# Attention scores in seven blocks of 64 rows with both heads stacked, in a kernel of causal attention and a gated product

## The chip, the cores and the metric

The kernel runs on one core of a Trainium2 chip. The metric is device time in microseconds (us) of one execution; the median of several runs counts. The core has TensorE (PE in the rows; its weight loads are PEld), VectorE (DVE), ScalarE (ACT), GpSimd (POOL) and a queue that issues the DMA transfers (SP).

## What is computed

Causal attention over 4 batches, 12 heads, 448 positions and 64 columns a head; its output, 768 columns a position, goes through a gated product.

```python
# q, k, v: (4, 12, 448, 64)
scores = np.matmul(q, k.transpose(0, 1, 3, 2)) / np.sqrt(64)
scores = np.where(np.triu(np.ones((448, 448), bool), k=1), -1e9, scores)
scores = scores - scores.max(-1, keepdims=True)
attn = np.exp(scores); attn = attn / (attn.sum(-1, keepdims=True) + 1e-9)
x = concat_heads(np.matmul(attn, v))              # (4 * 448, 768)
out = ((x @ w_a) * (x @ w_b)) @ w_out             # w_a, w_b: (768, 1536)
```

## The kernel before

**Numbers.** Everything is float32 at the output. Attention uses float32 matmuls. In the gated product each operand is split into a high and a low part and three products are summed (w_hi x_hi, w_hi x_lo, w_lo x_hi), each of 128 x 448 (line 586, 2484 of them in all). Weights arrive as 64-bit numbers and are converted by VectorE and ScalarE (lines 319 to 331), a unit of 128 x 768 at a time, then split (w_hi, w_lo).

**Order of the work.** The program is planned in one list of operations with estimated durations; a list scheduler (`Plan`) emits them in its own order, and each engine then runs its queue strictly in that order. First come batches 0 and 1, twelve pairs of heads (two heads share the 128 partitions of q and k, 64 each), with a few weight conversions in between. Each pair ends with `x_hi` (ScalarE) and `x_lo` (VectorE), its 128 rows of x. Then the products of batches 0 and 1 run, and the attention of batches 2 and 3, again twelve pairs, is set between them, a pair for every 30 groups of three products. Last come the products of batches 2 and 3, in a form with seven block products in place of eight; at that time the rooms of the attention (p, pt and others) hold parts of x.

**One pair.** `scores` makes, for each head, four row blocks: rows 0 to 63 against 64 columns, then three of 128 rows against 192, 320 and 448 columns (starts `QS`, ends `QE`). The two heads of a step are two matmuls on the two row halves of TensorE (64 rows each, 128 columns of weights), into two banks: s0 and s1 for the blocks of 448 and 64 columns, two m banks (batches 0 and 1) or t0 and t1 (batches 2 and 3) for 320 and 192. VectorE scales, adds the mask, writes to P and takes the row maximum in one instruction (line 409), ScalarE takes the exponential with its row sum (line 415). The sums go through an addition and a reciprocal on VectorE (lines 429 and 432), four of each a pair in batches 0 and 1 (`APART`), one of each later, on 128 x 8. P is then multiplied with them on GpSimd in batches 0 and 1 (line 442), on ScalarE later. The statistics have two tiles each, one a pair.

`turn` transposes P for one head: ten 128 x 128 pieces (line 464), in two banks t0 and t1, each then copied to a `pt` tile by ScalarE or VectorE (lines 268, 276). Where the diagonal piece's halves lie swapped, the `swapped` identity undoes it. `values` multiplies with V (line 484): four steps a head, weights of 64 columns, both heads at once on two column halves, into the bank pv.

**Rooms.** P lies in three rooms `p0` to `p2` of 128 x 1280, one a head. There are six `pt` tiles, four a pair; three V tiles; four tiles `raw` for q and k. The moving operands of the products are set 16 elements into their tiles (`SHIFT`).

**Start.** `START = "0w1ww"` orders the first loads: pair 0, a weight unit, pair 1, two units. Fillers (line 821) keep TensorE busy up to the first scores.

Of the kernel before, what the change touches and what calls it, by code (L numbers as in the profile page):

```python
# [18 lines left out]
P = 128  # L19
# [9 lines left out]
SHIFT, LINE = 16, 64  # L29

QS = (0, 64, 192, 320)
QE = (64, 192, 320, 448)
PO = (0, 128, 384, 768)
PW = 1280
NEG = -8.0e9

APART = (3, 3, 0, 0)
# [13 lines left out]
START = "0w1ww"  # L51
# [168 lines left out]
def causal_attention_then_gated_product(  # L220
# [18 lines left out]
    def shifted(tag, n, count, width):  # L239
        return plan.ring(tag, n, lambda i: sbuf.tile([P, LINE + count * width], F32R, tag=f"{tag}{i}", name=f"{tag}{i}")[  # L240
            :, SHIFT:SHIFT + count * width].rearrange("p (k f) -> p k f", k=count))
# [14 lines left out]
    sm_buf = [const.tile([P, 2, 4], F32, name=f"sm{i}") for i in range(2)]  # L256
# [34 lines left out]
    nth = [0, 0, 0]  # L291
# [80 lines left out]
    def scores(b, hp):  # L372
        qk_t = qk.pop((b, hp))
        sm = plan.ring("sm", 2, None)
        sm.tile = sm_buf[hp % 2]
        nm, rc = sb("nm", 2, [P, 2, 4]), sb("rc", 2, [P, 2, 4])
        for j in range(2):
            p = plan.ring("p", NPB, None)
            p.tile = p_buf[nth[0] % NPB]
            nth[0] += 1  # L380
            p_of[b, hp, j] = p

        def chunk(p, i):
            r = D if i == 0 else P
            return p.t[:r, PO[i]:PO[i] + QE[i]]

        for pair, w0 in (((3, 0), 448), ((2, 1), 320)):

            banks = [bank(f"s{j}") if w0 == 448 else bank("m", 3) if b < 2 else bank(f"t{j}") for j in range(2)]
            at = {pair[0]: slice(0, w0), pair[1]: slice(w0, 512)}  # L390
            for i in pair:

                def mm(i=i, banks=banks, at=at):
                    for j in range(2):
# [4 lines left out]
                    return r  # L399

                plan.op("pe", pe_ns(QE[i], 4) + 60, mm, [(qk_t, 0), (qk_t, 1)], banks)
            for j in range(2):
                p = p_of[b, hp, j]
                for i in pair:
                    r = D if i == 0 else P

                    def negmax(i=i, j=j, p=p, r=r, bk=banks[j], at=at):
                        m = mask[:r, 320:384] if i == 0 else mask[:, S - QE[i]:]
                        return nc.vector.tensor_tensor_reduce(  # L409
                            out=chunk(p, i), in0=bk.t[:r, at[i]], in1=m, scale=-0.125, scalar=3.0e38,  # L410
                            op0=ALU.add, op1=ALU.min, accum_out=nm.t[:r, j, i:i + 1],
                        )

                    def exp(i=i, j=j, p=p, r=r):
                        return nc.scalar.activation(  # L415
                            chunk(p, i), chunk(p, i), AF.Exp, bias=nm.t[:r, j, i:i + 1], scale=-1.0,
                            accum_out=sm.t[:r, j, i:i + 1],
                        )

                    plan.op("dve", dve_ns(QE[i]) + 10, negmax, [banks[j], "mask"], [(p, i), (nm, j, i)])  # L420
                    plan.op("act", act_ns(QE[i], False, 2), exp, [(nm, j, i)], [(p, i), (sm, j, i)])
        pairs = {slice(0, 4): (3, 0, 2, 1)}
        if APART[b] & 2:
            pairs = {slice(0, 4, 3): (3, 0), slice(1, 3): (2, 1)}
        heads = {slice(j, j + 1): (j,) for j in range(2)} if APART[b] & 1 else {slice(0, 2): (0, 1)}
        for si, ci in pairs.items():
            for sj, cj in heads.items():
                n = len(ci) * len(cj)
                plan.op("dve", 69 + n, lambda sj=sj, si=si: nc.vector.tensor_scalar_add(  # L429
                    rc.t[:, sj, si], sm.t[:, sj, si], 1.0e-9),  # L430
                    [(sm, j, i) for j in cj for i in ci], [(rc, j, i) for j in cj for i in ci])
                plan.op("dve", 115 + n, lambda sj=sj, si=si: nc.vector.reciprocal(  # L432
                    rc.t[:, sj, si], rc.t[:, sj, si]), [], [(rc, j, i) for j in cj for i in ci])
        for ci in pairs.values():
            for j in range(2):
                for i in ci:
                    def norm(i=i, j=j, p=p_of[b, hp, j]):
                        s = rc.t[:D if i == 0 else P, j, i:i + 1]
                        pc = chunk(p, i)
                        if NORM[b] == "act":  # L440
                            return nc.scalar.activation(pc, pc, AF.Copy, scale=s)
                        return nc.gpsimd.tensor_scalar(  # L442
                            out=pc, in0=pc, scalar1=s, scalar2=1.0, op0=ALU.mult, op1=ALU.mult
                        )

                    ns = act_ns(QE[i]) if NORM[b] == "act" else pool_ns(QE[i])
                    plan.op(NORM[b], ns, norm, [(rc, j, i)], [(p_of[b, hp, j], i)])


    spots = (((3, 448), (0, 0)), ((2, 320), (1, 0)))  # L450

    def turn(b, hp, j):
        p = p_of.pop((b, hp, j))
        for n, spot in enumerate(spots):
            t = bank(f"t{n}")
            for c, o in spot:
                for i in range(c, 4):


                    swap = c == i and c in (1, 2)  # L460
                    at = o + QS[i] - 128 * c + (D if swap else 0)

                    def mm(c=c, i=i, swap=swap, at=at, t=t):
                        return nc.tensor.matmul(  # L464
                            t.t[:, at:at + P],
                            p.t[:, PO[i] + 128 * c:PO[i] + 128 * (c + 1)],
                            swapped if swap else ident, is_transpose=True, start=True, stop=True,
                        )

                    plan.op("pe", 109, mm, [(p, i), "ident"], [t])  # L470
            full = sb("pt", 6, [P, 512])
            copy(TAKE[b][n], 512, lambda full=full: full.t, lambda t=t: t.t, [t], [full], True)
            pt[j, n] = full

    def values(b, hp, x):
        ps, vt = bank("pv"), v_of.pop((b, hp))
        parts = dict(pt)
        for c in range(4):
            n = 0 if c in (0, 3) else 1
            o = dict(spots[n])[c]  # L480

            def mm(c=c, n=n, o=o):
                for j in range(2):
                    r = nc.tensor.matmul(  # L484
                        ps.t[j * D:(j + 1) * D, 128 * c:S], vt.t[:, c, j, :],
                        parts[j, n].t[:, o:o + S - 128 * c], start=c == 0, stop=c == 3,
                    )
                return r

            plan.op("pe", pe_ns(S - 128 * c, 4) + 60, mm,  # L490
                    [(vt, 1 if c == 3 else 0), parts[0, n], parts[1, n]], [ps])
# [17 lines left out]
    def places(tag, n, take, count, width):  # L509

        at = SHIFT if tag == "pt" else LINE - SHIFT
        t = plan.ring(tag, n, lambda i: sbuf.tile([P, width], F32R, tag=f"{tag}{i}", name=f"{tag}_x{i}"))
        return [((lambda c=c: t.t[:, at + c * S:at + (c + 1) * S]), (t, c)) for c in range(take)]

    def make_rooms():
# [5 lines left out]
        block["T2"] = [[*places("p", 3, 2, 2, PW), *places("pt", 6, 1, 1, 512)] for _ in range(2)]  # L521
        block["T4"] = [[*places("p", 3, 2, 2, PW), *places("pt", 6, 1, 1, 512)]]

    def more_rooms():
        block["T4"].append(places("w_64", 3, 3, 3, 2 * UW))
        block["T3"] = [places("w_64", 3, 3, 3, 2 * UW) for _ in range(2)]
# [49 lines left out]
    def part_g(b, f, g, key):  # L576
        b, f = b % 2, f % HF
        copy("act", S, lambda: g_hi[:, b, f, :], g, [key], [("g_hi", b, f)])
        two_input("dve", S, lambda: g_lo[:, b, f, :], g,
                  lambda: g_hi[:, b, f, :].bitcast(F32), ALU.subtract, [key, ("g_hi", b, f)], [("g_lo", b, f)])  # L580
# [227 lines left out]
    for t in sm_buf:  # L808
        nc.vector.memset(t, 1.0)
# [72 lines left out]
```

## Time and profile before

| | |
|---|---|
| median of 3 runs | 677.49 us (677.25 to 677.79) |
| the profiled execution | 679.13 us |
| its span | 677.4 us |
| PE busy | 666.7 us (98%) |
| DVE busy | 474.7 us (70%) |
| ACT busy | 365.6 us (54%) |
| POOL busy | 56.0 us (8%) |
| chain that ended last | PE 90%, DVE 5%, ACT 3%, POOL 2% |

The span is what the rows add up to; the execution's own time has 1.7 us around it. Matmul records overlap, since they are pipelined, so a busy PE is not PE at its peak: its work is read from start to start. The same holds for short instructions of VectorE, whose records overlap by some tens of ns. Shapes stand as partitions x columns, out first; a matmul of float32 counts as two records.

### The profile page before, as it was taken

How to read it: one execution, taken by the hardware profiler on the slowest of the kernel's cores; microseconds unless marked ns; L12 is line 12 of the kernel's file. 1: busy time of each engine (PE TensorE's matmuls, PEld its weight loads, DVE VectorE, ACT ScalarE, POOL GpSimd, SP SyncE). 2: the span in 40 equal slices, each digit the busy share in tenths (PEclk: the TensorE clock that was granted, in tenths of full speed). 3: DMA queues.
4: the chain of work that ended last, by engine and by line, in shares of the span. 5: the costliest groups of instructions: out<-in, count | busy, mean ns of one | idle time of the engine just before them, and what ended most of it. 6: DMA issues, size and time to landing. Idle time of an engine off the chain costs nothing.

```text
span 677.4 us, 10680 instructions
## 1 busy us (share of the span) xinstructions
PE 666.7 (98%) x3754; PEld 578.6 (85%) x3754; DVE 474.7 (70%) x1122; ACT 365.6 (54%) x886; POOL 56.0 (8%) x107
## 2 busy tenths in 40 slices
PE   8999999999999999999999999999999999999997
PEld 6665568898898889889889889999999999999997
DVE  6889898898976665576767697478864237886521
ACT  5787767667657747757756753244432334343200
POOL 4455650000000000000000000000000000000000
PEclk9999999999999999999999999999999999999999
DMA  8335445657554764643542156412223231222542
GB/s 305 120 86 176 108 144 178 219 172 251 196 187 145 264 233 165 223 163 112 179 160 85 54 171 208 139 47 71 59 61 132 101 116 48 70 54 79 165 122 95
DMA packets 41716, 95.84 MB, mean 141 GB/s; under 512 B 4800, under 2 KB 27840, under 8 KB 41664
## 3 DMA queue, kind: packets, MB, share of 16 engines
q1 hardware_dynamic: 41664, 95.18, 42.5%
q8 instruction: 29, 0.48, 0.3%
q14 instruction: 23, 0.19, 0.1%
HBM read 67.24 MB, written 27.92 MB: 140 GB/s over the span
## 4 chain that ended last, share of the span: by engine, by line
PE 90%; DVE 5%; ACT 3%; POOL 2%; issue 1%; POOLq 0%; ACTq 0%
PE m L586 73%; PE t L464 6%; PE pv L484 4%; PE s L396 3%; ACT p L415 2%; DVE p L409 2%; POOL p L442 2%; PE t L396 2%; PE fill L821 1%; DVE pt L276 1%; DVE rc L429 1%; PE m L396 1%; ACT pt L268 1%; DVE w_m L321 0%; DVE rc L432 0%
## 5 line engine op out<-in xcount | busy, mean ns | idle before, releaser
L586 PE MATMUL m<-x_hi,w_hi 128*128 128x448 f32 x432 | 160.3, 371 | 0.0
L586 PE MATMUL m<-x_lo,w_hi 128*128 128x448 f32 x432 | 156.4, 362 | 0.0
L586 PE MATMUL m<-x_hi,w_lo 128*128 128x448 f32 x432 | 156.2, 362 | 0.0
L415 ACT ACTIVATE p<-p,nm 128x448 f32<-128x448 f32 (+1 forms) x192 | 95.0, 497 | 37.1 <-DVE nm L409 37.1
L284 DVE TENSOR_TENSOR w_lo<-w,w_hi 128x768 fp32r<-128x768 f32 (+1 forms) x84 | 65.8, 784 | 61.2 <-ACT w_hi L268 60.2
L586 PE MATMUL m<-g_hi,w_hi 128*128 128x448 f32 x288 | 105.3, 366 | 0.0
L586 PE MATMUL m<-g_lo,w_hi 128*128 128x448 f32 x288 | 104.3, 362 | 0.0
L586 PE MATMUL m<-g_hi,w_lo 128*128 128x448 f32 x288 | 104.0, 361 | 0.0
L268 ACT ACTIVATE w_hi<-w 128x768 fp32r<-128x768 f32 (+1 forms) x84 | 59.2, 704 | 67.8 <-PE m L586 54.8
L586 PEld LDWEIGHTS m<-x_hi,w_hi 128*128 128x128 f32 x432 | 81.1, 188 | 6.7 <-issue 0.9
L586 PEld LDWEIGHTS m<-x_hi,w_lo 128*128 128x128 f32 x432 | 80.9, 187 | 5.9
L586 PEld LDWEIGHTS m<-x_lo,w_hi 128*128 128x128 f32 x432 | 81.1, 188 | 4.5
L268 ACT ACTIVATE mid<-m 128x448 f32<-128x448 f32 x72 | 38.9, 540 | 80.4 <-PE m L586 67.6
L464 PE MATMUL t<-ident,p 128*128 128x128 f32 x384 | 65.9, 282 | 4.0 <-ACT pt L268 2.4
L284 DVE TENSOR_TENSOR mid<-m,acc 128x448 f32<-128x448 f32 x48 | 29.9, 624 | 45.5 <-PE m L586 45.1
L464 PEld LDWEIGHTS t<-ident,p 128*128 128x128 f32 x384 | 47.3, 142 | 14.1 <-POOL p L442 5.5
L586 PEld LDWEIGHTS m<-g_hi,w_hi 128*128 128x128 f32 x288 | 54.1, 188 | 3.9
L586 PEld LDWEIGHTS m<-g_hi,w_lo 128*128 128x128 f32 x288 | 53.9, 187 | 3.9
L442 POOL TENSOR_SCALAR p<-p,rc 128x320 f32<-128x320 f32 (+2 forms) x96 | 53.1, 569 | 45.2 <-ACT p L415 24.9
L586 PEld LDWEIGHTS m<-g_lo,w_hi 128*128 128x128 f32 x288 | 54.1, 188 | 3.0
L268 ACT ACTIVATE pt<-t 128x512 f32<-128x512 f32 x72 | 41.6, 594 | 24.4 <-PE t L464 24.1
L484 PEld LDWEIGHTS pv<-pt,v 128*64 128x64 f32 x384 | 25.8, 136 | 25.6 <-issue 17.2
(83 smaller groups left out, 982.0 us busy)
## 6 DMA issues: line engine op xcount, KB each, us to landing
w<-w SPq DMA_DIRECT2D x36, 768.0 KB, 4.5
w_keep<-w SPq DMA_DIRECT2D x36, 384.0 KB, 2.7
w<-w_keep SPq DMA_DIRECT2D x36, 384.0 KB, 3.0
raw<-qT SPq DMA_DIRECT2D x24, 224.0 KB, 3.1
raw<-kT SPq DMA_DIRECT2D x24, 224.0 KB, 3.4
o_keep<-mid SPq DMA_DIRECT2D x24, 224.0 KB, 2.1
acc<-o_keep SPq DMA_DIRECT2D x24, 224.0 KB, 2.7
out<-mid SPq DMA_DIRECT2D x24, 224.0 KB, 1.9
```

The source lines that it names most:

```text
L268: return nc.scalar.activation(o(), i(), AF.Copy)
L276: return nc.vector.tensor_copy(o(), i())
L284: plan.op(engine, ns, lambda: e.tensor_tensor(out=o(), in0=a(), in1=b(), op=op), reads, writes)
L396: r = nc.tensor.matmul(banks[j].t[:, at[i]], q[:, QS[i]:QS[i] + P], k[:, 0:QE[i]], start=True, stop=True)
L409: return nc.vector.tensor_tensor_reduce(out=chunk(p, i), in0=bk.t[:r, at[i]], in1=m, scale=-0.125, scalar=3.0e38, op0=ALU.add, op1=ALU.min ...
L415: return nc.scalar.activation(chunk(p, i), chunk(p, i), AF.Exp, bias=nm.t[:r, j, i:i + 1], scale=-1.0, accum_out=sm.t[:r, j, i:i + 1],)
L429: plan.op("dve", 69 + n, lambda sj=sj, si=si: nc.vector.tensor_scalar_add(rc.t[:, sj, si], sm.t[:, sj, si], 1.0e-9), [(sm, j, i) for j in ...
L442: return nc.gpsimd.tensor_scalar(out=pc, in0=pc, scalar1=s, scalar2=1.0, op0=ALU.mult, op1=ALU.mult)
L464: return nc.tensor.matmul(t.t[:, at:at + P], p.t[:, PO[i] + 128 * c:PO[i] + 128 * (c + 1)], swapped if swap else ident, is_transpose=True, ...
L484: r = nc.tensor.matmul(ps.t[j * D:(j + 1) * D, 128 * c:S], vt.t[:, c, j, :], parts[j, n].t[:, o:o + S - 128 * c], start=c == 0, stop=c == 3,)
L586: r = nc.tensor.matmul(ps.t[:, :S], a[:, i, :], x(), start=first and n == 0, stop=last and n == 2, skip_group_check=part)
L821: nc.tensor.matmul(fill[:, 0:S - SHIFT], warm[:, 0:P], warm[:, at:at + S - SHIFT], start=True, stop=True)
```

## The change

**Scores.** A pair has seven blocks of 64 rows, r = 0 to 6, with 64 (r + 1) columns. Both heads of a block are stacked: one head's 64 rows in partitions 0 to 63, the other's in 64 to 127 (swapped in odd blocks). Blocks are made two at a time, (6, 5), then 0 alone, in s0 and s1; then (4, 3) and (2, 1) in two other banks. A step of two blocks is four matmuls, on four 64 x 64 quadrants of TensorE. Row maximum, exponential and normalisation then take both heads in one instruction, seven of each a pair instead of eight; the statistics lie in one tile `st`, and there is one addition and one reciprocal a pair everywhere.

**Transposes.** A 128 x 128 piece holds both heads: 16 a pair instead of 20, in four banks as before; the copies write the two heads apart.

**Rooms.** P has one room of 128 x 2048 a pair. In batches 0 and 1 there are four, two of which lie where g_hi lies later (`early`); `close_front` makes the first writers of g_hi wait for the users of all four. Then there are two. `pt` has three tiles of twice the size. SHIFT is gone.

**Start.** Three pairs are loaded first, then three weight units; the fillers are float32 matmuls of 128 columns.

```diff
-START = "0w1ww"
+START = "012www"
...
-    NPB, NVB = 3, 3
+    NPB, NPF, NVB = 2, 4, 3
+    st_buf = [sbuf.tile([P, 3, 8], F32, tag=f"st{i}", name=f"st{i}") for i in range(2)]
...
-    g_hi = const.tile([P, 2, HF, S], F32R, name="g_hi")
+    early = sbuf.tile([P, 2 * HF * S], F32, tag="g_hi", name="early")
+    g_room = Buf(lambda: sbuf.tile([P, 2, HF, S], F32R, tag="g_hi", name="g_hi"), [])
...
+    def p_room(b):
+        if b < 2:
+            p = plan.ring("front", NPF, None)
+            n = (front[1][0] - 1) % NPF
+            p.tile = p_buf[n] if n < NPB else early[:, (n - NPB) * PW:(n - NPB + 1) * PW]
+        else:
             p = plan.ring("p", NPB, None)
...
-                def mm(i=i, banks=banks, at=at):
-                    for j in range(2):
-                        q, k = (qk_t.t[j * D:(j + 1) * D, h] for h in range(2))
-                        r = nc.tensor.matmul(
-                            banks[j].t[:, at[i]], q[:, QS[i]:QS[i] + P], k[:, 0:QE[i]], start=True, stop=True
-                        )
+                def mm(rs=rs, at=at):
+                    for r in rs:
+                        for j in range(2):
+                            to = j if r % 2 == 0 else 1 - j
+                            q, k = (qk_t.t[j * D:(j + 1) * D, h] for h in range(2))
+                            x = nc.tensor.matmul(at[r][0].t[to * D:(to + 1) * D, at[r][1]],
+                                                 q[:, r * D:(r + 1) * D], k[:, 0:D * (r + 1)], start=True, stop=True)
...
+        plan.op("dve", 165, lambda: nc.vector.tensor_scalar_add(st.t[:, rc, 0:NR], st.t[:, sm, 0:NR], 1.0e-9),
+                [(st, sm, r) for r in rows], [(st, rc, r) for r in rows])
...
+    groups = (((0, 0, 7), (3, 7, 1)), ((1, 0, 5), (2, 5, 3)))
+
+    def turn(b, hp, n):
+        p = p_of[b, hp]
+        full = sb("pt", 3, [P, 2, 8, D])
+        places = [(c, r) for c, o, count in groups[n] for r in range(2 * c, NR)]
+        for h in range(2):
+            t = bank(f"t{h}")
+            for i, (c, r) in enumerate(places[4 * h:4 * h + 4]):
...
+                        t.t[:, P * i:P * (i + 1)], p.t[:, PO[r] + P * c:PO[r] + P * (c + 1)],
+                        swapped if r % 2 else ident, is_transpose=True, start=True, stop=True,
...
-        nc.tensor.matmul(fill[:, 0:S - SHIFT], warm[:, 0:P], warm[:, at:at + S - SHIFT], start=True, stop=True)
+    plan.filler = lambda: nc.tensor.matmul(fill[:, 0:P], warm, warm, start=True, stop=True)
```

In the program's order, TensorE's scores of a pair of batch 2, between products, stood like this before (s and t are banks, raw is the tile of q and k; the last word is the shape of weights' rows and moving columns):

```order
L396 MATMUL s_1669<-raw_1036 128x448
L396 MATMUL s_1671<-raw_1036 128x448
L396 MATMUL s_1669<-raw_1036 128x64
L396 MATMUL s_1671<-raw_1036 128x64
L396 MATMUL t_1677<-raw_1036 128x320
L396 MATMUL t_1679<-raw_1036 128x320
L396 MATMUL t_1677<-raw_1036 128x192
L396 MATMUL t_1679<-raw_1036 128x192
```

The same scores on TensorE with the change; each row stands for the two heads:

```order
L413 MATMUL s_1536<-raw_950 64x448 x2
L413 MATMUL s_1539<-raw_950 64x384 x2
L413 MATMUL s_1536<-raw_950 64x64 x2
L413 MATMUL t_1546<-raw_950 64x320 x2
L413 MATMUL t_1549<-raw_950 64x256 x2
L413 MATMUL t_1546<-raw_950 64x192 x2
L413 MATMUL t_1549<-raw_950 64x128 x2
```

Eight matmuls on row halves became fourteen on quadrants, and both heads of a block now go to one bank.

TensorE in batches 0 and 1, before: all ten transposes of a head (t from p) stand together, then a block of V products (pv) of the same pair.

```order
L464 MATMUL t_887<-ident,p_70 128x128 x5
L464 MATMUL t_898<-swapped,p_70 128x128
L464 MATMUL t_898<-ident,p_70 128x128
L464 MATMUL t_898<-swapped,p_70 128x128
L464 MATMUL t_898<-ident,p_70 128x128 x2
L484 MATMUL pv_907<-pt_869,v_76 64x448
L484 MATMUL pv_907<-pt_896,v_76 64x448
```

The same place with the change, from the second transposes of a pair on, with the scores (s, m) of the pair after it between them:

```order
L460 MATMUL t_701<-swapped,p_72 128x128
L460 MATMUL t_701<-ident,p_72 128x128
L460 MATMUL t_701<-swapped,p_72 128x128
L413 MATMUL s_726<-raw_438 64x448 x2
L413 MATMUL s_729<-raw_438 64x384 x2
L460 MATMUL t_738<-ident,p_72 128x128
L460 MATMUL t_738<-swapped,p_72 128x128
L413 MATMUL s_726<-raw_438 64x64 x2
L413 MATMUL m_745<-raw_438 64x320 x2
L413 MATMUL m_748<-raw_438 64x256 x2
L460 MATMUL t_738<-ident,p_72 128x128 x2
```

The kinds of work change more often. On VectorE in batches 0 and 1, before, ten rows in a row hold six of the small operations on the sums (rc, lines 429 and 432) between row maxima (line 409, ISA):

```order
L429 TENSOR_SCALAR rc_667<-sm_75 128x2
L409 ISA p_69,nm_735<-m_672,mask 128x320
L409 ISA nm_735 128x1
L432 RECIPROCAL rc_667<-rc_667 128x2
L429 TENSOR_SCALAR rc_667<-sm_75 128x2
L409 ISA p_69,nm_735<-m_672,mask 128x192
L409 ISA nm_735 128x1
L432 RECIPROCAL rc_667<-rc_667 128x2
L429 TENSOR_SCALAR rc_667<-sm_75 128x2
L432 RECIPROCAL rc_667<-rc_667 128x2
```

With the change there is one of each for a pair (lines 435 and 437 on st), and the first row maximum of the pair after next, here 448 columns into st_69, stands behind the reciprocal of st_69's last user, with seven normalisations on GpSimd in between:

```order
L437 RECIPROCAL st_69<-st_69 128x7
L422 ISA early,st_70<-s_394,mask 128x64
L422 ISA st_70 128x1
L422 ISA early,st_70<-m_419,mask 128x320
L422 ISA st_70 128x1
L272 COPY pt_432<-t_434 128x2x256
L422 ISA early,st_70<-m_422,mask 128x256
L422 ISA st_70 128x1
L422 ISA early,st_70<-m_419,mask 128x192
L422 ISA st_70 128x1
L422 ISA early,st_70<-m_422,mask 128x128
L422 ISA st_70 128x1
```

So the small operations went from eight a pair to two, and a wait for GpSimd came in front of each pair's first row maximum.

## Rows read from the trace of the kernel before

**Rows 1.** Windows by stage: us from:to, length, busy us (instructions) of each engine, clock, DMA share, GB/s.
```profile
0.00:136.00 136.00, 129.00 (x850) 91.70 (x851) 116.38 (x418) 95.29 (x294) 56.02 (x107) 0.99 0.52 167
136.00:270.00 134.00, 134.00 (x773) 117.72 (x772) 100.29 (x208) 91.11 (x214) 0.00 (x0) 1.00 0.59 202
...
530.00:677.00 147.00, 143.65 (x719) 134.33 (x717) 77.44 (x139) 42.47 (x81) 0.00 (x0) 1.00 0.30 96
```

**Rows 2.** Windows of 10 us from 20 to 110: one of nine, and their sum.
```profile
80.00:90.00 10.00, 8.90 (x53) 5.81 (x54) 7.92 (x30) 6.50 (x21) 6.81 (x13) 0.83 0.66 188
...
sum 90.00, PE 85.59 PEld 56.97 DVE 80.13 ACT 64.79 POOL 46.52; mean PE 9.51 PEld 6.33 DVE 8.90 ACT 7.20 POOL 5.17
```

**Rows 3.** Chain of waits in one period after 109 us: start, us, what.
```profile
109.15 15.21 PE m L586 x75
124.35 1.09 PE t L464 x10
...
129.56 1.12 PE s L396 x8
130.68 0.92 PE t L396 x8
131.60 1.88 PE pv L484 x16
133.48 15.21 PE m L586 x75
```

**Rows 4.** The same chain at 87 us: ten transposes behind a V product.
```profile
87.53 1.88 PE pv L484 x16
89.42 1.24 PE t L464 x10
```

**Rows 5.** Timeline of VectorE at 52 us: start, record's length, line, operation, tiles, shapes.
```profile
52.15 0.61 DVE L409 CUSTOM_DVE_ANT_0 p<-s,mask 128x448 f32<-128x448 f32 x1
...
52.69 0.21 DVE L409 CUSTOM_DVE_ANT_0 p<-s,mask 64x64 f32<-64x64 f32 x1
...
52.83 0.61 DVE L409 CUSTOM_DVE_ANT_0 p<-s,mask 128x448 f32<-128x448 f32 x1
...
53.52 0.48 DVE L409 CUSTOM_DVE_ANT_0 p<-m,mask 128x320 f32<-128x320 f32 x1
...
53.93 0.68 DVE L276 COPY pt<-t 128x512 f32<-128x512 f32 x1
...
54.53 0.34 DVE L409 CUSTOM_DVE_ANT_0 p<-m,mask 128x192 f32<-128x192 f32 x1
...
54.81 0.16 DVE L429 TENSOR_SCALAR rc<-sm 128x2 f32<-128x2 f32 x1
54.88 0.48 DVE L409 CUSTOM_DVE_ANT_0 p<-m,mask 128x320 f32<-128x320 f32 x1
```

**Rows 6.** Groups by form, VectorE: small operations, 20 to 110 us, then of the whole run.
```profile
L429 DVE TENSOR_SCALAR rc<-sm 128x2 f32<-128x2 f32 x40 | 10.1, 263 | 2.4 <-ACT p L415 2.2
...
L432 DVE RECIPROCAL rc<-rc 128x2 f32<-128x2 f32 x40 | 6.0, 157 | 0.4
...
L432 DVE RECIPROCAL rc<-rc 128x8 f32<-128x8 f32 x12 | 2.4, 201 | 0.3
...
L429 DVE TENSOR_SCALAR rc<-sm 128x8 f32<-128x8 f32 x12 | 2.0, 167 | 6.6 <-ACT p L415 6.6
```

**Rows 7.** Instructions that write x_lo, 0 to 110 us: shortest/median/longest ns, first and last start.
```profile
L284 DVE TENSOR_TENSOR x_lo<-pv,x_hi x12: 598/611/625, 20.9 to 108.5; 128x448 fp32r<-128x448 f32 x12
```

**Rows 8.** The page's group of normalisations on GpSimd: busy us, mean ns.
```profile
L442 POOL TENSOR_SCALAR p<-p,rc 128x320 f32<-128x320 f32 (+2 forms) x96 | 53.1, 569 | 45.2 <-ACT p L415 24.9
```

**Rows 9.** The page's products on the low parts of x and of g.
```profile
L586 PE MATMUL m<-x_lo,w_hi 128*128 128x448 f32 x432 | 156.4, 362 | 0.0
...
L586 PE MATMUL m<-g_lo,w_hi 128*128 128x448 f32 x288 | 104.3, 362 | 0.0
```

More of the change, by code (lines that the diff above doesn't have):

```diff
@@ L27 @@
 HF = FT // 2
[L29 to L34, printed above, removed]
+NR = S // D
+PO = tuple(128 * sum(n // 2 + 1 for n in range(r)) for r in range(NR + 1))
+PW = PO[NR]
+FIRST, SECOND = ((6, 5), (0,)), ((4, 3), (2, 1))
 NEG = -8.0e9
-APART = (3, 3, 0, 0)
 NORM = ("pool", "pool", "act", "act")
@@ L370, in load_pair @@
         qk[b, hp] = t
[L372 to L376, printed above, removed]
-        for j in range(2):
+    front = plan.rings["front"] = ([None] * NPF, [0])
+    def p_room(b):
[4 more added lines that the diff above has]
+        else:
             p = plan.ring("p", NPB, None)
@@ L422, in scores @@
[L422 to L447, printed above, removed]
@@ L450, in causal_attention_then_gated_product @@
[L450 to L473, printed above, removed]
+        return p
@@ L478, in values, with mm @@
         for c in range(4):
-            n = 0 if c in (0, 3) else 1
-            o = dict(spots[n])[c]
-            def mm(c=c, n=n, o=o):
+            n, (o, count) = next((n, g[1:]) for n in range(2) for g in groups[n] if g[0] == c)
+            def mm(c=c, n=n, o=o, count=count):
                 for j in range(2):
@@ L485, in mm @@
                         ps.t[j * D:(j + 1) * D, 128 * c:S], vt.t[:, c, j, :],
[L486 removed]
+                        parts[n].t[:, j, o:o + count, :].rearrange("p i d -> p (i d)"), start=c == 0, stop=c == 3,
                     )
@@ L507, in causal_attention_then_gated_product, with places @@
     block = {}
-    def places(tag, n, take, count, width):
-        at = SHIFT if tag == "pt" else LINE - SHIFT
+    def places(tag, n, take, width):
         t = plan.ring(tag, n, lambda i: sbuf.tile([P, width], F32R, tag=f"{tag}{i}", name=f"{tag}_x{i}"))
-        return [((lambda c=c: t.t[:, at + c * S:at + (c + 1) * S]), (t, c)) for c in range(take)]
+        return [((lambda c=c: t.t[:, c * S:(c + 1) * S]), (t, c)) for c in range(take)]
     def make_rooms():
@@ L520, in make_rooms @@
                                for x in (hi, lo)]
-        block["T2"] = [[*places("p", 3, 2, 2, PW), *places("pt", 6, 1, 1, 512)] for _ in range(2)]
-        block["T4"] = [[*places("p", 3, 2, 2, PW), *places("pt", 6, 1, 1, 512)]]
+        one, two = (places("p", NPB, 4, PW) for _ in range(2))
+        more = [places("pt", 3, 1, 1024) for _ in range(1)]
+        block["T2"] = [one[0:3], two[0:3]]
+        block["T4"] = [[one[3], two[3], *more[0]]]
     def more_rooms():
-        block["T4"].append(places("w_64", 3, 3, 3, 2 * UW))
-        block["T3"] = [places("w_64", 3, 3, 3, 2 * UW) for _ in range(2)]
+        block["T4"].append(places("w_64", 3, 3, 2 * UW))
+        block["T3"] = [places("w_64", 3, 3, 2 * UW) for _ in range(2)]
     def split_block(name, k, i, key):
@@ L742, in uses @@
                     if kind == "o":
-                        products(ps, parts[k // 3], k % 3, lambda k=k, b=b: g_hi[:, b % 2, k, :],
+                        products(ps, parts[k // 3], k % 3, lambda k=k, b=b: g_room.t[:, b % 2, k, :],
                                  lambda k=k, b=b: g_lo[:, b % 2, k, :],
```

122 lines of the change are left out of this document (74 added, 48 removed).

## The prediction

> **What bounds the kernel now.** I read the windows by stage first [rows 1]. From about 109 us on, TensorE is busy all the time (134.00 of 134.00 us in the second stretch); VectorE and ScalarE have slack there (100.29 and 91.11). So in what I call the path, 109 us to the end, the time is TensorE's own work, and only what shortens that work moves the end. Then the chain of waits from 109 us on [rows 3]: it names nothing but TensorE, with a period of 24.33 us for each pair of heads of batches 2 and 3 (109.15 to 133.48). A period holds products, ten transposes a head at 1.09 us (109 ns each), a block of scores of 1.12 + 0.92 = 2.04 us, and the product with V, 1.88 us. There are twelve such periods.
>
> Before 109 us lies what I call the front: the 12 pairs of batches 0 and 1, whose attention must be done before most products can start. The last step of each pair is x_lo; the first of the twelve starts at 20.9 us and the last at 108.5 [rows 7], so 11 pairs take 87.6 us, 7.96 each. VectorE is busy 80.13 us of the 90 from 20 to 110, ScalarE 64.79, GpSimd 46.52 [rows 2]. TensorE shows 85.59, but matmul records overlap, so I sum its work instead: a pair is 20 x 0.109 + 2.04 + 1.88 = 6.1 us [rows 3]. Where transposes, scores and V products are interleaved there is also a cost for each change between them: ten transposes right behind a V product take 1.24 us, against 1.09 behind a product [rows 3, 4], so 0.15 at most; I take 0.12. The order of instructions has 68 such changes in its first 11 pairs, of which two a pair are in the 2.04 and 1.88; the other 46 cost 5.5 us. With the 33 products that the order places there (0.203 each, 15.21 / 75) TensorE's work is 11 x 6.1 + 5.5 + 6.7 = 79.3 of 87.6 us. In 80 to 90 us its granted clock averages 0.83 [rows 2], which is a third of that stretch at 1.2 GHz and costs about 1.7 us more. So in the front two engines, VectorE and TensorE, are both at some 90%, and each waits for the other through three rooms for P that hold one head each, that is one pair and a half.
>
> **The change, part by part.**
>
> Transposes: 16 a pair instead of 20. In the path that is 4 x 0.109 x 12 = 5.2 us, with nothing beside it that could become later: the other engines lose work too.
>
> Scores on quadrants: the longest block of each step now sets 448 + 64 + 320 + 192 = 1024 columns, the same as before for one head, if four quadrants run at once. The weights are 64 columns wide instead of 128. The trace has no block on four quadrants. The nearest row is the V product: 64-wide weights, the same 1024 columns, two at a time, 1.88 us against 2.04 [rows 3]. I take 1.88, so 0.16 x 12 = 1.9 us; the lower end is no gain, the upper a loss (below, as a rival).
>
> VectorE in the front: each row-maximum costs, from its start to the next start [rows 5], 0.54 us at 448 columns, 0.41 at 320, 0.28 at 192, 0.14 at 64. Two heads of four were 2.74. The line through these is 0.075 + 1.04 ns a column; seven blocks with 1792 columns in all give 2.39, so 0.35 less. The additions and reciprocals fall from 8 to 2 a pair: by their records in the front (263 and 157 ns each) that is 1.68 to about 0.37 (the later forms' 167 and 201) [rows 6], 1.3 less; by start-to-start, 0.07 for the one at 54.81 [rows 5], only 0.4. I take 0.75. Copies (four a pair, now with a strided read) and x_lo stay. So 1.1 us x 11 = 12 us of VectorE's 80.
>
> TensorE in the front: 11 x (16 x 0.109 + 1.88 + 1.88) = 60.5. But the new order is chopped finer: 96 changes instead of 68, so 74 beyond the two a pair, 8.9 us. It places 39 products ahead of the last x_lo, 7.9. Sum 77.3, 2 us less than before.
>
> Rooms: four a pair instead of one and a half, so a pair's scores need not wait for the transposes of the pair ahead. This takes away the reason for which both engines stood at 90%. VectorE alone would give 87.6 x 68/80 = 74.5, a gain of 13 us; TensorE's 77.3 at its present share (79.3 + 1.7 of 87.6, 92.5%) gives 83.6, a gain of 4, and at 100% a gain of 10. I take 80.1, **7.5 us less** (TensorE at 96.5%), nearer to TensorE's row because it is now the longer sum. Bounds: no gain to 13.
>
> Since six more products stand ahead of the last x_lo, the path is 6 x 0.203 = 1.2 us shorter.
>
> Edits that I cost at nothing. The loads in another order: the weights land after three pairs, but their first use stands behind the row-maxima of six pairs; pair 3's q and k now queue behind three weight loads, at most some 3 us once, while three pairs lie ahead of them. Normalising on GpSimd: 7 instead of 8 of 569 ns [rows 8], 4.0 us a pair of more than 7. The wait of g_hi for the front's rooms: its first writer comes after a whole block of products. Fillers and memsets: they lie ahead of the first scores, which wait for a load. The tiles without the 16-element shift: products on shifted x and on unshifted g have the same mean, 362 ns [rows 9]; one nanosecond in each of the kernel's 2484 products would be 2.5 us either way. VectorE's and ScalarE's savings in the path: TensorE covers them.
>
> **Sum.** From the span of 677.4: - 5.2 - 1.9 - 7.5 - 1.2 = 661.6. The profiled run took 679.13 us with its surroundings, 1.7 more than its span; the median of the plain runs is 677.49, 0.1 above the span. So I expect a median of **661.5**.
>
> **Rivals.**
>
> (1) *The quadrants don't run four at once.* What speaks against it: in the trace two row halves (the scores) and two column halves (the V product) do run together, which is why blocks of 2 x 1024 columns take 2.04 and 1.88 us. What speaks for it: no row shows both splits together. If only two run, a pair's scores take 1792 columns instead of 1024; the streaming part is 1.88 - 0.13 = 1.75, so + 1.31 a pair. Path: 12 x 1.31 - 7.1 = + 8.6. Front: TensorE 77.3 + 11 x 1.31 = 91.7 at 96.5% is 95, + 7.4; with the 1.2, **692, slower**. It decides from some 0.65 us a pair on: 15.8 gained over 12 in the path and about 12 in the front. A second form: two heads that write one bank run one after the other, 2048 columns, + 1.75 a pair: path + 13.9, front (96.6 / 0.965 = 100) + 12.5, **703**.
>
> The Trainium skill, TensorEngine Tiling (Array Packing), section "Gotcha 1: PSUM Pressure", says that different row tiles cannot access one PSUM bank at the same time. Before, the two heads' scores went to two banks; here both heads of a block go to the two partition halves of one bank, so by that rule the second form would hold and the time be 703. The trace has no two row halves in one bank, so it neither bears it out nor refutes it; I give that form 5%, as the halves never share a partition of the bank.
>
> (2) *The front gains nothing.* Statistics (st) still have two tiles, one a pair: the first row-maximum of pair n + 2 stands in VectorE's queue and waits for the last of seven normalisations of pair n, which cannot start before the one reciprocal of all seven blocks. That is 7 x 0.569 = 4.0 us [rows 8] plus hand-overs, while only 2 to 2.5 us of VectorE's work stand between that reciprocal and that row-maximum; copies for the pair ahead are queued behind the wait, and TensorE's V product waits for those. A loop of 4.0 + 0.6 + 1.5 = 6.1 us a pair (hand-overs and the work up to the next reciprocal estimated from [rows 5]) is still under 7.3, which speaks against it; another 1.2 us anywhere in it and the front stands at 8 again. Time: 677.4 - 5.2 - 1.9 - 1.2 = **669**.
>
> (3) *The front runs at VectorE's pace*, 74.5 us: 677.4 - 8.3 - 13 = **656**. Against it stands TensorE's 77.3, unless a change of block costs less than 0.12.
>
> **How the numbers follow.** Forecast with its band of 657 to 666: 55%. Rival 3, and a little below it: 14%. Rival 2, 667 to 674: 18%. Something within 0.2% of now (a front that loses what the path gains): 3%. Rival 1: 10%, half in each form. The range is 652 to 673: it takes in no gain in the scores, a front from 0 to 13 us and 2 us for the products; outside are rival 1, the last 2% above 673, some 3% below 652 and the 3% of no change. A measurement here tells 0.2%, about 1.4 us, from no change. Faster 0.87, same 0.03, slower 0.10.
>
> **What would show it.** In the path the period of 24.33 us should fall to about 23.7: 16 transposes at 109 ns, scores at 1.88. If scores take 3.2 or 3.6 there, rival 1 holds. The last x_lo should start near 101 us; at 108 rival 2 holds, and VectorE's waits for GpSimd ahead of a row-maximum should show; below 96 rival 3. The granted clock should not fall in the front. The prediction is wrong at its root if TensorE has idle stretches after the last x_lo, for lack of converted weights.

## The result, and the profile after

The changed kernel takes 670.86 us (median of four runs, 670.37 to 671.33) against 677.64 for the kernel before (677.25 to 678.61): a ratio of 0.9898, with a 95% interval of 0.9881 to 0.9915. The forecast was a gain of 16 us; the gain is 6.8. The profiled execution took 670.64 us with a span of 668.9, so what lies around the span is 1.7 us, as before.

The forecast's sum starts from the profiled execution of the kernel before, which at 679.13 us was 1.6 us longer than the median of its plain runs (of 27 more runs beside the experiments, 4 took 679.1 to 679.4 us and the others 676.9 to 678.1), so that span against span the change is -8.5 us (677.4 to 668.9) and median against median -6.8.

I read the trace of after in the order in which I had read that of before. First the windows by stage (us from:to, length, busy us and instructions of PE, PEld, DVE, ACT, POOL, clock, DMA share, GB/s), to be held against [rows 1, 2]:

```profile
20.00:110.00 90.00, 87.02 (x711) 52.24 (x710) 71.12 (x227) 65.74 (x197) 41.30 (x72) 1.00 0.46 144
...
136.00:270.00 134.00, 134.00 (x852) 114.62 (x851) 100.52 (x209) 86.55 (x206) 0.00 (x0) 1.00 0.64 212
```

TensorE is still busy all the time in the path. In the window of the front VectorE's 80.13 us have become 71.12, and the clock no longer falls there. The instructions that write x_lo, 0 to 130 us, answer to [rows 7]:

```profile
L280 DVE TENSOR_TENSOR x_lo<-pv,x_hi x12: 605/615/625, 20.4 to 101.3; 128x448 fp32r<-128x448 f32 x12
```

The front is 80.9 us (20.4 to 101.3) where it was 87.6. What VectorE waits for in it, by line (busy us, mean ns, then idle us before it and what ended that):

```profile
L272 DVE COPY pt<-t 128x512 f32<-128x512 f32 x22 | 15.2, 690 | 10.7 <-PE t L460 10.6
```

It waits for TensorE's transposes, 10.6 of the 10.7 us ahead of 22 copies. TensorE in its turn is not quite without idle time; from 20 to 101 us it waits 2.8 us, each time for a normalisation on GpSimd (us in total, times, longest):

```profile
PE t L460 <- POOL early L442: 2.2, 4, 0.7
PE t L460 <- POOL p L442: 0.6, 1, 0.6
```

VectorE waits nowhere for GpSimd in that window. Then the chain of waits over one period of the path (start, us, what), which answers to [rows 3]:

```profile
124.42 15.40 PE m L581 x75
139.81 0.87 PE t L460 x8
...
144.59 0.96 PE s L413 x8
145.54 0.05 PE t L413
145.60 0.01 PE s L413
145.60 0.87 PE t L413 x12
146.47 1.88 PE pv L478 x16
148.35 15.40 PE m L581 x75
...
220.17 15.69 PE m L581 x75
...
387.08 278.07 PE m L581 x1371
```

A pair's transposes are two times 0.87 us (109 ns each), its scores 0.96 + 0.05 + 0.01 + 0.87 = 1.89 us, which is what the forecast had. But the period is 23.93 us (148.35 - 124.42), not 23.7: 75 products take 15.40 us where they took 15.21. They are the same instructions. And it is not one rate: of the eleven blocks of 75 in the chain seven take 15.40 us, and every second one from 220 us on, four in all, takes 15.69. The page's groups say the same (busy us, mean ns of one), against 362 in [rows 9]:

```profile
L581 PE MATMUL m<-x_lo,w_hi 128*128 128x448 f32 x432 | 157.8, 365 | 0.0
...
L581 PE MATMUL m<-g_lo,w_hi 128*128 128x448 f32 x288 | 105.3, 365 | 0.0
```

On the mean a product's record is some 3 ns longer, and there are 2484 products. So the question for the chip was: what slows an instruction that the change does not touch?

### The profile page after: what moved, and what is told of

Read it like the earlier page. It is cut to its first block, busy times and chain, and to the rows that moved or that the text cites. A ratio compares the mean times of both kernels' runs of the same rounds, so it can differ in the third digit from the quotient of the medians.

```text
span 668.9 us, 10897 instructions
## 1 busy us (share of the span) xinstructions
PE 659.9 (99%) x3956; PEld 559.8 (84%) x3956; DVE 453.7 (68%) x1005; ACT 349.0 (52%) x826; POOL 49.8 (7%) x104
## 4 chain that ended last, share of the span: by engine, by line
PE 95%; POOL 3%; DVE 1%; POOLq 0%; issue 0%; ACT 0%
PE m L581 76%; PE t L460 7%; PE pv L478 5%; PE s L413 3%; POOL early L442 2%; PE t L413 2%; PE m L413 2%; POOL p L442 1%; PE fill L816 1%; POOLq L871 0%; DVE pt L272 0%; DVE p L422 0%; DVE w L327 0%; ACT w_hi L264 0%; DVE mid L280 0%
## 5 line engine op out<-in xcount | busy, mean ns | idle before, releaser
L581 PE MATMUL m<-x_hi,w_lo 128*128 128x448 f32 x432 | 157.9, 366 | 0.0
L428 ACT ACTIVATE p<-p,st 128x384 f32<-128x384 f32 (+6 forms) x126 | 62.4, 497 | 23.8 <-DVE st L422 23.6
L478 PE MATMUL pv<-pt,v 128*64 128x448 f32 (+3 forms) x384 | 49.5, 389 | 0.0
L460 PE MATMUL t<-ident,p 128*128 128x128 f32 x180 | 38.8, 279 | 0.9 <-DVE pt L272 0.7
L280 DVE TENSOR_TENSOR mid<-m,mid 128x448 f32<-128x448 f32 x36 | 22.5, 625 | 23.5 <-PE m L581 23.2
```

The source lines that it names most:

```text
L280: plan.op(engine, ns, lambda: e.tensor_tensor(out=o(), in0=a(), in1=b(), op=op), reads, writes)
L428: return nc.scalar.activation(view(r), view(r), AF.Exp, bias=st.t[:, nm, r:r + 1], scale=-1.0, accum_out=st.t[:, sm, r:r + 1],)
L460: return nc.tensor.matmul(t.t[:, P * i:P * (i + 1)], p.t[:, PO[r] + P * c:PO[r] + P * (c + 1)], swapped if r % 2 else ident, is_transpose= ...
L478: r = nc.tensor.matmul(ps.t[j * D:(j + 1) * D, 128 * c:S], vt.t[:, c, j, :], parts[n].t[:, j, o:o + count, :].rearrange("p i d -> p (i d)" ...
L581: r = nc.tensor.matmul(ps.t[:, :S], a[:, i, :], x(), start=first and n == 0, stop=last and n == 2, skip_group_check=part)
```

## The experiments

**Where the tiles lie.** The change also moves tiles in SBUF. The program as built gives these start addresses modulo 256 bytes. Before: the product's weights (w_hi, w_lo) at 0, all its moving operands (x, g, and the parts of x that lie in other tiles) at 64; for x that is what SHIFT did. After: everything at 64; the statistics tiles that lie ahead of the weights take 192 bytes where 128 stood before. Theory A: a product's rate depends on the distance from the weights' start to the moving operand's, which was 64 and is now 0. The first four experiments undo that alone, bring it alone into the kernel before, keep the distance and move both, and take another distance. Padding tiles that nothing reads, or another order of tiles, do it.

First, e1_w0: the weights alone back at 0.

```diff
+    const.tile([P, 48], F32, name="pad_a")
     w_hi = const.tile([P, 18, P], F32R, name="w_hi")
     w_lo = const.tile([P, 18, P], F32R, name="w_lo")
+    const.tile([P, 16], F32, name="pad_b")
```

> The changed kernel, with 48 unused words set ahead of the product weights w_hi and w_lo and 16 behind, so that these start at 0 modulo 256 bytes, as before the change, and not at 64; every other tile stays at the same offset, and the order of instructions is the same. In the changed kernel a product takes 15.40 us / 75 = 205 ns against 203 before, over 2484 products some 6 to 7 us. Theory A (the offset of the weights against the moving operands, now the same 64 for both, sets the rate): products back at 203, time 664. Theory B (the weights' own offset sets it, whatever the moving operands have): also 664. Theory C (the rate comes from something else, such as the traffic of the other engines): 671.

Measured: 662.98 us (662.53 to 664.05), 0.9787 [0.9771, 0.9803] of before; span 660.9. Its chain of waits:

```profile
123.62 15.21 PE m L583 x75
...
143.59 0.95 PE s L415 x8
144.54 0.05 PE t L415
144.59 0.01 PE s L415
144.60 0.87 PE t L415 x12
...
147.35 15.21 PE m L583 x75
```

Its x_lo:

```profile
L282 DVE TENSOR_TENSOR x_lo<-pv,x_hi x12: 607/614/625, 19.8 to 100.7; 128x448 fp32r<-128x448 f32 x12
```

And its page's products:

```profile
L583 PE MATMUL m<-x_lo,w_hi 128*128 128x448 f32 x432 | 156.3, 362 | 0.0
...
L583 PE MATMUL m<-g_lo,w_hi 128*128 128x448 f32 x288 | 104.3, 362 | 0.0
```

And the last piece of products in its chain:

```profile
382.75 274.43 PE m L583 x1371
```

The 75 products are at 15.21 again, in every one of the eleven blocks, the scores are untouched, the period is 23.73, and 7.9 us are back (670.86 - 662.98). Of the 8.0 us between the two spans, 3.6 lie in the last 1371 products (278.07 - 274.43), 3.5 between the starts of the blocks at 124 and 387 us, and the rest before, of which 0.6 ahead of the first x_lo (20.4 against 19.8), where no product has run yet. So 7.4 us can be the products', 3.0 ns each.

Second, e2_bw64: the kernel before, with its small tiles of sums put ahead of the weights, which moves, of the products' operands, only those (to 64).

```diff
+    sm_buf = [const.tile([P, 2, 4], F32, name=f"sm{i}") for i in range(2)]
     w_hi = const.tile([P, 18, P], F32R, name="w_hi")
     w_lo = const.tile([P, 18, P], F32R, name="w_lo")
-    sm_buf = [const.tile([P, 2, 4], F32, name=f"sm{i}") for i in range(2)]
```

> The kernel before, with the two small statistics tiles (64 bytes) set ahead of w_hi and w_lo instead of behind, so that the weights start at 64 modulo 256 like the moving operands; nothing else moves. Theories A and B: products 205 ns instead of 203, time 684. Theory C: 677.6.

Measured: 684.17 us (683.21 to 684.35), 1.0094 [1.0079, 1.0109]: 6.8 us slower than the kernel before (677.36 beside it). Its chain:

```profile
132.56 15.40 PE m L586 x75
```

The loss of the change appears in the old kernel by itself, so it has nothing to do with quadrants, rooms or transfers.

Third, e3_all0: the changed kernel with 48 words ahead of the rooms of P and all that lies behind them, so that weights and moving operands all start at 0.

```diff
+    sbuf.tile([P, 48], F32, tag="pad", name="pad")
     p_buf = [sbuf.tile([P, PW], F32, tag=f"p{i}", name=f"p{i}") for i in range(NPB)]
```

> The changed kernel, with 48 unused words ahead of all its tiles, so that weights and moving operands both start at 0 modulo 256. Theory A: still 205 ns and 671, since the two offsets are the same. Theory B: 203 ns and 664, since the weights are at 0. Theory C: 671.

Measured: 670.36 us, 0.9892 [0.9875, 0.9909]. Its chain:

```profile
124.52 15.40 PE m L582 x75
```

With the weights at 0 but the distance 0, nothing is won, and the longer blocks of 15.69 us stand in the same four places as in after. It is not the weights' own place.

Fourth, e4_w128: weights at 128, moving operands at 64 (distance -64, that is 192).

```diff
+    const.tile([P, 16], F32, name="pad_a")
     w_hi = const.tile([P, 18, P], F32R, name="w_hi")
     w_lo = const.tile([P, 18, P], F32R, name="w_lo")
+    const.tile([P, 48], F32, name="pad_b")
```

> The changed kernel, with 16 unused words ahead of w_hi and w_lo and 48 behind: weights at 128 modulo 256, moving operands at 64. Theory A (only equal offsets are slow): 203 ns and 664. Theory B (only 0 is fast): 205 ns and 671. Theory C: 671.

Measured: 668.06 us (667.89 to 668.78), 0.9861 [0.9847, 0.9876]. Its chain:

```profile
124.67 15.37 PE m L583 x75
```

That is neither of the times expected, 664 and 671, but lies between them. So theory A does not hold in the form that only equal places are slow, nor theory B, that only weights at 0 are fast.

**How the rate goes with the distance.** Three more kernels changed only the sizes of the two pads (32 and 32 words; 56 and 8; and 16 and 48 on top of e3_all0).

e5_w192: weights at 192, moving operands at 64 (distance 128).

> The changed kernel with 32 unused words ahead of w_hi and w_lo and 32 behind: weights at 192 modulo 256 bytes, moving operands at 64, so the moving operands start 128 behind the weights. So far: 64 behind is fast (663 and, in the kernel before, 677.4), equal is slow (670.4 to 670.9, 684.2), 192 behind in between (668.1). Theory A1 (only equal offsets collide fully, half of it at 192): 663 to 665. Theory A2 (the rate falls the further the offset is from 64): 665 to 671.

Measured: 672.81 us (672.51 to 672.91), 0.9927 [0.9913, 0.9942]. Its chain:

```profile
124.72 15.49 PE m L583 x75
```

Both forms of the theory that I had for this run miss (663 to 665, 665 to 671): the time does not fall or rise steadily with the distance.

e10_w64m0: weights at 64, moving operands at 0, the distance of e4_w128 in other absolute places.

> The changed kernel with the product's weights at 64 and all moving operands at 0 (start addresses modulo 256 bytes): moving less weights is -64, that is 192 modulo 256, the same as in the fourth experiment (weights 128, moving 64; 668.1 us) with other absolute places. Theory A (only the difference counts): 667.5 to 668.7, products of 204.9 ns (75 in 15.37 us). If the distance counts without its sign (64 either way), as in the first experiment: 663, products of 203 ns. If the absolute places count as well, any other time between 663 and 673.

Measured: 668.82 us (667.86 to 669.22), 0.9862 [0.9843, 0.9881]. Its chain:

```profile
125.08 15.37 PE m L584 x75
```

The same 15.37 and, within 1 us, the same time as e4_w128; it is 0.1 us above the time expected. At a distance of 192 as at 0 (after and e3_all0) only the difference counts, and its sign counts too: -64 is not 64.

e11_w32: weights at 32 (distance 32).

> The changed kernel with the product's weights at 32 and all moving operands at 64 (modulo 256 bytes): a difference of 32, half of what the first experiment has. What the time does between a difference of 0 (670.4 to 670.9) and of 64 (663.0) is open. A grain of 64 bytes: as 0, 670 to 671, or as 64, 663. Without a grain: about 667, in the middle.

Measured: 676.07 us (675.05 to 676.47), 0.9974 [0.9964, 0.9983]: nearly the whole gain of the change is lost. Its chain:

```profile
125.02 15.68 PE m L583 x75
```

None of the three expectations held; a distance of 32 is not between 0 and 64 but worse than both. In order of time, with the changed kernel's work: distance 64, 663.0 us (15.21 for 75 products); 192, 668.1 and 668.8 (15.37); 0, 670.4 and 670.9 (15.40, some 15.69); 128, 672.8 (15.49); 32, 676.1 (15.68). The kernel before was at the best of the five. The last 1371 products come in the same order: 274.43 us at 64, 277.45 at 192, 278.07 at 0, 279.88 at 128, 280.50 at 32. Transposes, scores and V products last as long in all of them, but that tests nothing: the pads move no operand of theirs against the other. Two things stay open. Why the rate goes in this way is not settled; and the distance is not all, since at a distance of 0 blocks of 15.40 and of 15.69 us stand in one kernel.

**What the front's gain hangs on.** From here on e1_w0 is the base, so that the products are as before. e6_rooms2: two rooms for P in the front instead of four.

```diff
-    NPB, NPF, NVB = 2, 4, 3
+    NPB, NPF, NVB = 2, 2, 3
```

> The run e1_w0 (weights back at 0) with two rooms for P in batches 0 and 1 too, instead of four. Theory R (the depth of the rooms carries the front's gain of 7 us): last x_lo at 106 to 109 us and a time of 668 to 671. Theory L (the front is shorter because each pair costs the engines less, and rooms matter little): last x_lo at 101 to 103, time 663 to 665.

Measured: 670.78 us (668.77 to 670.99), 0.9892 [0.9872, 0.9911], 7.8 more than e1_w0 and within the 668 to 671 expected if the rooms carry the gain. Its x_lo:

```profile
L282 DVE TENSOR_TENSOR x_lo<-pv,x_hi x12: 615/624/626, 21.9 to 110.2; 128x448 fp32r<-128x448 f32 x12
```

Its windows at the first of two falls of the clock:

```profile
46.00:48.00 2.00, 1.65 (x11) 0.92 (x11) 1.87 (x5) 0.60 (x1) 0.71 (x1) 0.88 0.30 111
48.00:50.00 2.00, 2.00 (x9) 0.60 (x7) 2.00 (x8) 0.84 (x3) 2.00 (x6) 0.50 0.50 142
```

The last x_lo comes at 110.2, 1.2 us later still than expected, and the front is 88.3 us long, no shorter than before (87.6), although VectorE and TensorE have all their savings. With two rooms TensorE has gaps (1.65 of 2.00 us), and behind them the granted clock is 0.50, 1.2 GHz.

e7_start: the old order of loads.

```diff
-START = "012www"
+START = "0w1ww"
```

> The run e1_w0 with the loads ordered at the start as before the change (pair 0, a weight unit, pair 1, two units, pair 2). If the new order of loads is worth nothing, as I costed it: 663. If VectorE's first idle microseconds were bought off by the early second and third pair: 664 to 666, with the first x_lo at 20 to 22 us and the others later by 1 to 3 us.

Measured: 665.70 us (665.32 to 665.98), 0.9823 [0.9808, 0.9838], 2.7 more than e1_w0. Its x_lo:

```profile
L282 DVE TENSOR_TENSOR x_lo<-pv,x_hi x12: 607/614/625, 26.6 to 106.4; 128x448 fp32r<-128x448 f32 x12
```

Its chain at the start:

```profile
2.69 5.66 DMA w<-w
8.35 0.02 issue
8.37 7.32 DMA raw<-kT
15.69 0.14 issue
15.83 1.76 PE s L415 x6
```

And its windows there:

```profile
14.00:16.00 2.00, 1.20 (x7) 0.53 (x10) 0.37 (x2) 1.47 (x7) 1.49 (x3) 0.64 1.06 354
16.00:18.00 2.00, 2.00 (x11) 0.62 (x10) 0.34 (x1) 0.00 (x0) 1.92 (x5) 0.50 1.04 374
```

A pair's k lands at 15.69, behind a load of weights; TensorE's scores wait for it, and TensorE works on at 1.2 GHz (granted clock 0.50) when it has come. The time is as expected (664 to 666), the way there is not: the first x_lo was expected at 20 to 22 us and the others 1 to 3 us later, but the first comes at 26.6, 6.8 us later, and the last 5.7. Between them the front is not longer (79.8 us; 80.9 in e1_w0). The planner also sets 51 products ahead of the last x_lo instead of 39, 2.4 us of later work, so the span grows by 3.3 only (660.9 to 664.2). In this kernel, then, the new order of loads is worth 2.7 us; what it would be worth in the kernel before was not run.

e8_st4: four tiles of statistics instead of two, against rival 2.

```diff
-    st_buf = [sbuf.tile([P, 3, 8], F32, tag=f"st{i}", name=f"st{i}") for i in range(2)]
+    st_buf = [sbuf.tile([P, 3, 8], F32, tag=f"st{i}", name=f"st{i}") for i in range(4)]
+    sbuf.tile([P, 16], F32, tag="pad", name="pad")
...
-        st = plan.ring("st", 2, None)
-        st.tile = st_buf[nth[3] % 2]
+        st = plan.ring("st", 4, None)
+        st.tile = st_buf[nth[3] % 4]
```

> The run e1_w0 with four statistics tiles instead of two, so that the first row maximum of a pair no longer waits for the normalisations of the pair two ahead. Rival 2's mechanism (that wait holds the front): last x_lo 3 to 5 us earlier, time 658 to 660. TensorE holds the front (its own work and its changes of block): the same within 1 us, 662 to 664.

Measured: 662.10 us (661.63 to 662.21), 0.9768 [0.9751, 0.9785], 0.9 less than e1_w0 (662.98), as expected if that wait does not hold the front. Its x_lo:

```profile
L283 DVE TENSOR_TENSOR x_lo<-pv,x_hi x12: 614/624/625, 21.7 to 100.2; 128x448 fp32r<-128x448 f32 x12
```

Without the wait of a row maximum for the normalisations of two pairs ago, the last x_lo comes 0.5 us earlier, not 3 to 5, so that wait is not what holds the front at its length. But the first x_lo comes 1.9 us later here, and the front itself is 78.5 us long instead of 80.9, so up to 2.4 us may hang on it. And the run says nothing of the transposes, which also wait for normalisations (2.8 us in after).

**What four quadrants are worth.** e9_two: both heads' odd blocks go to the quadrants of the even ones, so that two are used instead of four.

```diff
-                            to = j if r % 2 == 0 else 1 - j
+                            to = j
...
-                        swapped if r % 2 else ident, is_transpose=True, start=True, stop=True,
+                        ident, is_transpose=True, start=True, stop=True,
```

> The kernel of the first experiment (weights at 0, all else at 64), but the blocks of scores with odd numbers are no longer swapped: both heads' odd blocks go to the same two quadrants as the even ones, so that only two of TensorE's four quadrants are used. This prices rival 1 of the prediction. Theory Q (four quadrants do run at once, and the trace's 1.88 us a pair is that): a pair's scores rise from 1.88 to about 3.2 us (1792 columns instead of 1024), 12 pairs in the path cost 15.7 us, and the front, which TensorE holds, up to 14.4 more: 679 to 693 us, so slower than the kernel before. Theory N (scores on quadrants run in some other way, and the split into four is worth nothing): 663, as the first experiment.

Measured: 691.26 us (690.41 to 691.78), 1.0194 [1.0175, 1.0213]: slower than the kernel before. Its chain:

```profile
139.80 15.21 PE m L583 x75
...
159.76 1.66 PE s L415 x12
161.42 1.52 PE t L415 x16
162.94 1.88 PE pv L480 x16
164.82 15.21 PE m L583 x75
```

Its x_lo:

```profile
L282 DVE TENSOR_TENSOR x_lo<-pv,x_hi x12: 610/618/626, 24.4 to 114.9; 128x448 fp32r<-128x448 f32 x12
```

Scores are 1.66 + 1.52 = 3.18 us a pair instead of 1.88. The period grows by 1.29 (25.02 against 23.73), 15.5 us over twelve, and the last x_lo comes 14.2 later (114.9 against 100.7); together 29.7, and the span grew by 29.1 (660.9 to 690.0).

**A faster version.** e12_costs: e1_w0 with two of the planner's costs nearer to the records.

```diff
-                plan.op("dve", dve_ns(n) + 70, negmax, [at[r][0], "mask"], [(p, r), (st, nm, r)])
-                plan.op("act", act_ns(n, False, 3), exp, [(st, nm, r)], [(p, r), (st, sm, r)])
+                plan.op("dve", dve_ns(n) + 10, negmax, [at[r][0], "mask"], [(p, r), (st, nm, r)])
+                plan.op("act", act_ns(n, False, 2), exp, [(st, nm, r)], [(p, r), (st, sm, r)])
```

> The kernel of the first experiment with two costs of the planner nearer to what the trace shows: a row maximum 60 ns less, an exponential's extra of three units only two. It moves instructions in the front alone to any extent. If TensorE's own work holds the front (as the experiment with four tiles of statistics says), the time stays within 2 us of 663: 661 to 665. If the order leaves a gap that the costs close: 655 to 661.

Measured: 660.45 us (659.59 to 661.80), 0.9743 [0.9720, 0.9765], the fastest here. Its x_lo:

```profile
L282 DVE TENSOR_TENSOR x_lo<-pv,x_hi x12: 615/624/625, 23.7 to 99.2; 128x448 fp32r<-128x448 f32 x12
```

And its window of the front:

```profile
20.00:110.00 90.00, 89.33 (x732) 54.77 (x729) 73.23 (x234) 66.77 (x200) 37.46 (x70) 1.00 0.47 147
```

TensorE is busy 89.33 of 90 us there (87.02 after), so a small gap in the order was left to close, as the expectation of 655 to 661 had it, by 0.5 us. Its waits for GpSimd from 20 to 101 us have gone from 2.8 us (after and e1_w0) to 0.4:

```profile
PE t L462 <- POOL p L444: 0.4, 1, 0.4
```

The front is 75.5 us long (23.7 to 99.2), 5.4 shorter than in e1_w0, of which three products fewer ahead of the last x_lo are 0.6. The first x_lo comes 3.9 us later, in an execution whose granted clock is 0.87 from 10 to 20 us and which, at 661.80, was the longest of the four, so most of the gain in the front does not show in the time.

## Why the prediction was wrong

The sign and the range held. The size did not, and one step accounts for it: **"the tiles without the 16-element shift"**, which stood among the edits costed at nothing, with "2 us for the products" in the range. It is a loss of 7.9 us (670.86 - 662.98); by the traces 7.4 of the 8.0 us between the spans are the products', 3.0 ns in each of 2484. It was not SHIFT's removal as such: e1_w0 has no SHIFT either, and its products are as fast as before. What cost the time is that the weights came to lie at 64. Two things went wrong in that step. [Rows 9] showed equal means for products on shifted x and on unshifted g, and I took that for a test of the shift; but what counts is the distance from weights to operand, and both x and g lay at 64 from weights at 0. Equal rows tested nothing. And I looked at what SHIFT did to the moving operands, not at the weights, which moved by 64 bytes because the small tiles ahead of them changed size.

With that one distance restored (e1_w0), the other steps can be read, span against span: forecast 677.4 to 661.6, measured 660.9.

- **Transposes and scores in the path** (5.2 + 1.9): right. A period falls from 24.33 to 23.73 us, 7.2 over twelve; transposes are 109 ns, scores 1.88 to 1.89 us.
- **The front** (-7.5 at the last x_lo): right in size, 108.5 to 100.7, that is -7.8; in the changed kernel itself -7.2. Of the 7.8, 6.7 lie between the first and the last x_lo (87.6 to 80.9; forecast 80.1) and 1.1 ahead of the first. The engine that I named, TensorE, is the one that VectorE waits for (10.7 us ahead of its copies). That the size came out so well is partly luck: TensorE's 2.8 us of waits for GpSimd are 3.5% of the 80.9, just the share left idle at 96.5%, but that share was chosen between two bounds and not worked out. And TensorE's sum of 77.3 us was no floor, since e12_costs runs the front in 75.5 with three products fewer (0.6). VectorE's busy time falls by 9.0 us in the window of 90 us (80.13 to 71.12), though the window's last 9 us are no longer front, so the forecast 12 can't be read off exactly; as VectorE isn't the bound, nothing hangs on it.
- **Rooms**: right in kind, and stronger than the text says. Without the third and fourth the whole gain of the front is gone (e6_rooms2, 7.8 us), whatever the engines save.
- **Loads** ("at most some 3 us once", costed at nothing): not nothing in this kernel, where the old order costs 2.7 us (e7_start). How much of that is in the 7.8 of the front is not shown, since the kernel before had the old order and its first x_lo at 20.9 us all the same, only 1.1 later than e1_w0; the gains of rooms and loads can't be added.
- **Six more products ahead** (1.2): the rest of the sum. -7.2 - 7.8 - 1.2 = -16.2, and the span of e1_w0 is 16.5 shorter.
- **From the span to the median**: a small miss. I put the median 0.1 above the span, from a profiled execution with a stretch at 1.2 GHz in it [rows 2], and counted that stretch as gained too. With the 1.7 us around the span the same sum gives 663.3; e1_w0 took 662.98.

The rivals. **Rival 1** (quadrants not four at once) fell: four run at once. Its price was right, though: 3.18 us a pair against the 3.19 of its sum (whose 0.13 us stands in no row), and 691.3 us where it said 692, which e9_two measured by using two quadrants. Its second form, from the Trainium skill (TensorEngine Tiling (Array Packing), "Gotcha 1: PSUM Pressure"), did not come about either: in the trace of after, matmuls of two row tiles with their outputs in the two partition halves of one bank take 1.89 us a pair, not the 3.6 that one after the other would take. Here the Trainium skill and the measurement differ, and the measurement decides for this case. **Rival 2**'s time (669) is close to what was measured, but not its mechanism: the last x_lo did not stay at 108, VectorE waits nowhere for GpSimd between 20 and 101 us, and e8_st4, which takes the wait away, gains 0.9 us, less than the 1.4 that can be told from no change. Whoever had looked at the time alone would have called it right. **Rival 3** (VectorE's pace) fell: last x_lo at 101.3, not below 96, and VectorE idle ahead of its copies.

## What to carry to other kernels

When a change adds or drops tiles or alters their sizes, list where the operands of the untouched, most frequent instruction start before and after, weights and moving operand both, and price a changed distance by the count of those instructions. Rows that are equal on two operands test a property only if the operands differ in it. And when a time comes out near a rival's, look for the rival's place in the trace before believing it: here the front did all it should, and the loss was in products that the change did not touch.

## What the runs showed of the hardware

Products of 128 x 448 in float32 with 128 x 128 weights depended on the distance between the start of the weights and of the moving operand, counted here modulo 256 bytes: 75 of them took 15.21 us at 64, 15.37 at 192, 15.40 or 15.69 at 0, 15.49 at 128 and 15.68 at 32, which is 13 us of the kernel's 663 between best and worst. At 0 and at 192 two pairs of absolute places gave the same. That 256 bytes are the period was not tested; other distances, shapes and types were not tried. For the other matmuls the distance changed only between the two kernels (transposes from 128 to 0, V products from 192 to 0, scores not at all), and they took 109 ns and 1.88 us both times. What in the chip makes the products' rate so, and why two rates occur at 0, is not shown.

Four 64 x 64 quadrants of TensorE ran at once, two heads writing the two partition halves of one bank: a pair's scores took 1.88 to 1.89 us on four quadrants and 3.18 on two.
